# Cluster-routed attention and a long convolution on one core: the output weights' load cut in four, three more idle products, two folded inverses, and a new order

## The chip, the core and the metric

The kernel runs on one core of a Trainium2 chip. Its engines are TensorE (PE, products; PEld are its weight loads), VectorE (DVE), ScalarE (ACT), GpSimd (POOL) and SyncE (SP, which here only issues DMAs). The metric is the device time of one execution in microseconds; lower is better. Every time below is of that kind, and the times inside an execution come from one profiled run.

## What is computed

Four batches, eight heads, 768 positions, 64 columns a head. Every query and key is assigned to one of 16 clusters of its head; a query attends only to keys of its own cluster. The attention's output, 512 columns a position, goes through a gated convolution over all positions:

```python
q_assign = argmax(einsum('bhsd,hcd->bhsc', q_n, c_n))     # q_n, c_n: normalised
k_assign = argmax(einsum('bhsd,hcd->bhsc', k_n, c_n))
mask = q_assign[:, :, :, None] == k_assign[:, :, None, :]
scores = where(mask, q @ k.T / 8, -1e9)
attn = softmax(scores) @ v                                # x[b, s, h*64+d]
x1, x2, x3 = split(x @ w_proj, 3)                         # 512 x 1536
x2_conv = irfft(rfft(x2, axis=1) * rfft(filter_fft, axis=0), axis=1)
y = x1 * x2_conv * x3
out = y @ w_out                                           # 512 x 512, float32
```

## The kernel before

**A planned order.** The kernel is not written in the order in which it runs. Every operation is recorded with `Plan.op` (L94): the engines that may do it with an estimated duration for each, a due time, the keys that it reads and writes, the PSUM bank that it takes or frees. `place` (L123) then puts the operations one by one on the engines: of those that are ready, by due time and estimated start. The table `NUDGE` (L43) holds a shift of the due time for each operation, by its number in the order of recording, and `ONLY` pins some operations to one engine. So these two tables, together with the estimates, set the order of every engine's instructions and of the DMA queues. `COLD` is a constant of the planner's estimates alone: it tells until when TensorE is reckoned to run slow.

**Groups and stages.** The work comes in eight head groups n, two a batch, four heads each. For each group:
- the loads of q and k (L323) and v (L328), by half groups (pair pr of two heads);
- `routing(n)` (L574): transposes of q and k on TensorE (L594, L605), similarities with the centroids (sim, L625) and their transpose (L638), the one-hot of the best cluster (L646 to L663), a DMA transpose of the one-hots (ohT, L668), and eight small DMAs that copy them as mask rows into the score operands (aug<-ohT, L497). The mask is thus part of the score product: a large constant times the one-hots is added in the contraction;
- `attention(n, pr)` (L677): for each of six key tiles three score products of 512 columns (L699, through `product`, L82 for whole 128-column products and L84 for two halves of 64), their exponentials on ACT (L708, L711), and the product with the values (L722). VectorE and POOL sum the exponentials over key tiles: first tiles two at a time (L739, 512 columns, on either engine), then whole tiles (L743, VectorE). The denominators are either a product with ones (L756), or a DMA that folds the sums (acc<-acc, L776, issued by POOL) and two small ones (dd, L780; dp, L782) ahead of a reciprocal and its spread over partitions (rb, L793). The result is scaled into x transposed (xT, L822).

After an odd group its batch is complete, and `hyena(b)` (L830) is recorded; its products fill TensorE between the scores of the next groups: the projection x2 (L856), sums of positions with their mirror (L870, L875), the spectra by products with DFT tables (L475, L84), the product with the filter's spectrum (L886, L890), and then for each of four column tiles dt the projections x3 and x1 (L919 to L930), the inverse transform (L939 to L952), the product y2 of the three (L968), and at last the product with the output weights (L994 to L1012) and the output DMAs (L988, L1007, L1011). The last batch's `hyena` has nothing behind it that could hide it: it is the tail.

**Two forms of the inverse.** A whole inverse takes 16 calls of `product`; its two halves of frequencies (even, odd) are combined inside PSUM, with a negated table `neg` (L894), and VectorE then makes two sums (yy, L965). A folded one takes 8; VectorE makes two sums more (sd, L955) before the two of L965. The copy od (L953) is there in both. `whole = last and dt >= WHOLE` (L898) decides; with `WHOLE = 0` all four of the last batch are whole, and the other batches' are folded.

**The head.** `warm` (L1089) fills a part of the tile wpj with ones and issues `WARM` idle products of 128x128 by 512 columns (L1096), which read nothing else and whose result nobody reads, before the first transposes (L605). `constants` (L1016) loads the DFT tables; the filter's spectrum hm is made on the way (L455 and around).

**The weights.** `weights` (L1078) records four loads of the projection (L1082) and one of the output weights (L1085), all issued by POOL. The tile wout is at first the third DFT table of the filter's spectrum, so its load waits for the last reader of `("fw", 2, ...)`.

**DMAs.** A queue issues in order; an issue whose data or buffer isn't ready holds up what stands behind it. SyncE's queue carries q, k, v, the one-hot transposes, the masks, dd, rb and the outputs; POOL's carries the weights and the folds acc<-acc.

Of the kernel before, what the change touches and what calls it, by code (L numbers as in the profile page):

```python
# [26 lines left out]
ND = DM // 128  # L27
# [10 lines left out]
WHOLE = 0  # L38
# [6 lines left out]
HOLD = {"score": "score", "o": "o"}  # L45
AFTER = {"PE": .16}
TABLE = 1.283
WARM = 7
SOON = 0
RATE = 215e3  # L50
LOAD = 300e3

COLD, SLOW = 6.5, .95
OVERLAP = {"ACT": .09, "DVE": .08}
MODES = {"pv": 64, "bc": 64, "half": 64, "sim": 32, "den": 32, "score": 0, "proj": 0, "inv": 0}


def array(o, last):

# [205 lines left out]
def build(T):  # L265

    P = Plan()
    op = P.op
# [406 lines left out]
    first, prev = [None], []  # L675

    def attention(n, pr, sins):  # L677
# [120 lines left out]
        else:  # L798
# [10 lines left out]
            for ch in range(2):  # L809
# [6 lines left out]
                op(("PE", .95), bc, te + 3, r=["dn"], w=[rk[ch]], alloc=rk[ch], kind="bc")  # L816
        osv = lambda: T.osb[o3][:, :, :384]
        eps = lambda: T.osb[o3][:, 1, 384:385]
        xs = b % 2
        xv = lambda: T.xT[xs][:, kt].rearrange("p (a b) -> p a b", a=2)  # L820
        for a_ in [slice(0, 2)] if not last else [slice(0, 1), slice(1, 2)]:
            op(("DVE", .6 if last else 1.01), lambda e, a_=a_: T.nc.vector.scalar_tensor_tensor(  # L822
                xv()[:, a_], osv()[:, a_], eps(), ap(rk[a_.start])[:, :384].unsqueeze(1) if last else rbv(), op0=Alu.add,
                op1=Alu.mult), te + (4 if last else 12), r=[("osb", o3)] + (rk[a_] if last else rk), w=[("xT", xs, kt)],
               free=rk[a_] if last else [], lock=True)


    INV = [("inv", m) for m in range(2)]

    def hyena(b):  # L830
        xs = b % 2
        last = b == B - 1
        w0 = A(24 * (b + 1)) + 11.84958
        w1 = A(24 * (b + 2)) + 50.56423 if b < B - 2 else A(96) + 35.31752
        if last:
            w0 = A(96) - 4.47412
            w1 = w0 + 10
        acc = [0.0]

        def step(d):  # L840
# [130 lines left out]
        for tt in range(3):  # L971
            ob, obk = (T_("tm", 0), [("tm", 0, 0), ("tm", 0, 1), ("tm", 0)]) if last and tt == 2 else (
                T_("ob", tt % 2), [("ob", tt % 2, 0), ("ob", tt % 2, 1), ("ob", tt % 2)])
            for e_ in range(2):
                due = step(.87)
                if last and tt == 2 and e_:
                    for x in range(2):
                        h, cols = Bank(), ts(x, DM // 2)

                        def half(e, kts, cols=cols, h=h):  # L980
                            for kt in kts:
                                columns(ap(h)[:, :DM // 2], T.y2[:, kt, ts(NT - 1, 128)], T.wout[:, kt, cols], kt == 0, kt == ND - 1)
                        op(("PE", .36), lambda e, half=half: half(e, range(3)), due, r=[("y2", dt) for dt in range(3)] + ["wout"],
                           w=[h], alloc=h, kind="proj")
                        op(("PE", .12), lambda e, half=half: half(e, range(3, 4)), due, r=[("y2", 3), h], w=[h], kind="proj")
                        op({"ACT": .37, "DVE": .42}, lambda e, cols=cols, ob=ob, h=h: copy(e, ob()[:, 1, cols], ap(h)[:, :DM // 2]), due + 1,
                           r=[h], w=[("end", x)], free=[h])
                        op({"ACT": .4, "SP": .4}, lambda e, cols=cols, ob=ob: dma(e)(  # L988
                            T.out[b].rearrange("(p t) m -> p t m", t=NT)[:, NT - 1, cols], ob()[:, 1, cols]), due + 2,
                           r=[("end", x)], byts=78e3)  # L990
                    break
                h = Bank()

                def W(e, kts=range(ND), tt=tt, e_=e_, h=h):  # L994
                    for kt in kts:
                        columns(ap(h), T.y2[:, kt, ts(2 * tt + e_, 128)], T.wout[:, kt], kt == 0, kt == ND - 1)
                if last:
                    op(("PE", .647), lambda e, W=W: W(e, range(3)), due, r=[("y2", dt) for dt in range(3)] + ["wout"],
                       w=[h], alloc=h, kind="proj")
                    op(("PE", .217), lambda e, W=W: W(e, range(3, 4)), due, r=[("y2", 3), h], w=[h], kind="proj")  # L1000
                else:
                    op(("PE", .862), W, due, r=[("y2", dt) for dt in range(ND)] + ["wout"], w=[h], alloc=h,
                       kind="proj")
# [74 lines left out]
    def weights():  # L1078
        op(("POOL", .1), lambda e: T.nc.gpsimd.tensor_copy(T.wpj[0:1, :, 0:1], T.f[1][0:1, 0, 0:4].unsqueeze(2)), 29,
           r=[("f", a, b) for a in range(2) for b in range(2)], w=[("wpj", i) for i in range(ND)])  # L1080
        for i in range(ND):
            op(("POOL", .8), lambda e, i=i: T.nc.gpsimd.dma_start(  # L1082
                T.wpj[:, i], T.w_proj.rearrange("(t p) m -> p t m", p=128)[:, i]), 44 + 13 * i, w=[("wpj", i)], byts=786e3,
               after=[first[0]], kind="load")
        op(("POOL", .8), lambda e: T.nc.gpsimd.dma_start(T.wout, T.w_out.rearrange("(t p) m -> p t m", p=128)), 115,  # L1085
           w=["wout", ("fw", 2, 0), ("fw", 2, 1)], byts=1048e3, after=[first[0]], kind="load")
# [188 lines left out]
```

## Time and profile before

| what | value |
|---|---|
| median of 3 runs | 380.7 us (376.28 to 382.66) |
| profiled execution, its own time | 378.68 us |
| its span in the trace | 376.9 us |
| granted TensorE clock, mean | 0.999 |
| busy: TensorE, VectorE | 363.4 us, 339.2 us |
| busy: ScalarE, GpSimd | 262.7 us, 108.5 us |
| last product ends, output DMAs end | 372.6 us, 376.9 us |
| first group of instructions on TensorE | the seven idle products, 1.45 to 4.62 us |

The span runs from the first to the last record of the trace; the execution's own time is 1.8 us longer. The costliest groups of instructions are the products with the values (L722, 143.1 us in 768 products), the halved products of L84 (69.4 us for the scores alone) on TensorE; the exponentials on ACT (L711 and L708, 109.1 and 57.5 us); and the sums L743 on VectorE (112.3 us in 64). In the lines of the trace an instruction is shown with its start, its duration, engine, line, operation, the tiles that it writes and reads, their shapes and a count, and in brackets the idle time ahead of it and what ended it. A matmul's end is modelled, so a stretch of idle time is read better from start to start.

### The profile page before, as it was taken

The page shows a single profiled execution, that of the slowest core. Times are in us where ns is not written, and L with a number is a line of the kernel's source. Part 1 is how long each engine was busy: PE and PEld are TensorE (multiplying, and loading weights), DVE is VectorE, ACT ScalarE, POOL GpSimd, SP SyncE. Part 2 cuts the span into 40 slices and gives each one's busy share as a digit, 9 for nine tenths or more (in the row PEclk, how much of TensorE's full clock was granted, in tenths as well). Part 3 has the DMA queues.
Part 4 walks back from the last instruction along what each step waited for, and adds up shares of the span by engine and source line. Part 5 has one row for each costly group of instructions (what it writes and reads, how often), then busy time and mean ns, then how long its engine had stood idle before and what let it go on. Part 6 is the DMA issues. An engine that isn't in the chain of part 4 may idle for free.

```text
span 376.9 us, 8462 instructions
## 1 busy us (share of the span) xinstructions
PE 363.4 (96%) x3240; PEld 207.4 (55%) x3242; DVE 339.2 (90%) x507; ACT 262.7 (70%) x490; POOL 108.5 (29%) x153
## 2 busy tenths in 40 slices
PE   7999999999999699999999999999999999999995
PEld 4554445454555355566555556667555565565682
DVE  7889996868899859999998988999899999999992
ACT  7996969786985567769669637889855876433332
POOL 8511102321221642331331144311330252022600
PEclk9999999999999999999999999999999999999999
DMA  8869756682587777869785796748355941120214
GB/s 171 186 122 209 129 129 165 120 193 50 115 178 106 176 147 133 130 127 181 157 114 136 129 208 137 142 98 128 63 77 101 210 85 13 45 101 2 113 57 167
DMA packets 95668, 47.56 MB, mean 126 GB/s; under 512 B 83768, under 2 KB 89612, under 8 KB 95628
## 3 DMA queue, kind: packets, MB, share of 16 engines
q1 hardware_dynamic: 91836, 37.69, 44.4%
q0 software_dynamic: 2704, 8.98, 17.0%
q8 instruction: 25, 0.41, 0.5%
q10 hardware_dynamic: 1088, 0.36, 0.4%
q14 instruction: 15, 0.12, 0.1%
HBM read 31.59 MB, written 7.40 MB: 103 GB/s over the span
## 4 chain that ended last, share of the span: by engine, by line
PE 75%; DVE 11%; DMA 6%; issue 3%; ACT 3%; SPq 2%; DVEq 0%; ACTq 0%
PE pair L722 27%; PE bank L84 27%; PE bank L82 5%; PE bank L856 4%; DVE acc L743 4%; PE bank L594 3%; PE bank L625 2%; DMA vraw<-in_v_dram 2%; PE bank L638 1%; PE bank L605 1%; DMA qkraw<-in_k_dram 1%; DMA rb<-dr 1%; PE bank L756 1%; DMA dd<-acc 1%; DVE hm L455 1%
## 5 line engine op out<-in xcount | busy, mean ns | idle before, releaser
L722 PE MATMUL pair<-p,vraw 128*64 128x385 f32 x768 | 143.1, 490 | 2.6 <-DMA vraw<-in_v_dram 2.5
L711 ACT ACTIVATE p<-bank 128x512 f32<-128x512 f32 x192 | 109.1, 606 | 29.7 <-PE bank L84 24.6
L743 DVE TENSOR_TENSOR acc<-p,acc 128x1536 f32<-128x1536 f32 x64 | 112.3, 1754 | 3.5 <-POOL acc L739 0.8
L722 PEld LDWEIGHTS pair<-p,vraw 128*64 128x64 f32 x768 | 54.8, 136 | 51.9 <-issue 41.7
L84 PE MATMUL bank<-aug,aug 80*64 80x256 bf16 (+3 forms) x626 | 69.4, 326 | 1.0 <-DMA aug<-ohT 0.5
L708 ACT ACTIVATE p<-bank 128x512 f32<-128x512 f32 x96 | 57.5, 606 | 7.7 <-PE bank L84 4.8
L84 PEld LDWEIGHTS <-aug 80*64 80x64 bf16 (+1 forms) x626 | 38.7, 109 | 33.5 <-issue 21.5
L776 POOL DMA_DIRECT2D acc<-acc x30 | 23.8, 792 | 95.3 <-DMA acc<-acc 53.9
L284 POOL CAST aug<-qkP 64x768 bf16<-64x768 f32 x28 | 23.2, 833 | 67.2 <-DVE acc L743 33.6
L84 PE MATMUL bank<-xT,wpj 128*64 128x384 bf16 x392 | 36.2, 326 | 0.0
L282 ACT COPY qkP<-bank 128x512 f32<-128x512 f32 (+1 forms) x46 | 23.6, 550 | 12.7 <-PE bank L594 6.5
L84 PEld LDWEIGHTS <-y 128*64 128x64 bf16 x504 | 24.8, 110 | 13.8 <-issue 5.5
L886 DVE TENSOR_TENSOR tm<-bank,hm 128x512 f32<-128x512 f32 x44 | 27.8, 682 | 4.7 <-PE bank L475 3.2
L890 POOL TENSOR_TENSOR y<-tm 128x512 bf16<-128x512 f32 x19 | 23.9, 1274 | 17.3 <-DVE tm L886 12.9
L84 PEld LDWEIGHTS <-wpj 128*64 128x64 bf16 x392 | 23.1, 110 | 10.4 <-issue 2.6
L739 DVE TENSOR_TENSOR acc<-p,p 128x512 f32<-128x512 f32 x38 | 24.9, 683 | 4.1 <-ACT p L708 2.7
L739 POOL TENSOR_TENSOR acc<-p,p 128x512 f32<-128x512 f32 x10 | 13.4, 1347 | 39.5 <-ACT p L711 25.5
L84 PE MATMUL bank<-wout,y 128*64 128x512 bf16 (+1 forms) x200 | 22.8, 370 | 0.0
L856 PE MATMUL bank<-wpj,xT 128*64 128x512 bf16 x192 | 22.1, 379 | 0.0
L282 ACT CAST aug<-qkP 64x768 bf16<-64x768 f32 x24 | 19.8, 830 | 2.3 <-PE bank L84 1.5
L282 ACT COPY ob<-bank 128x512 f32<-128x512 f32 x19 | 10.8, 591 | 13.2 <-PE bank L84 12.9
L746 ACT COPY osb<-pair 128x770 f32<-128x770 f32 x16 | 12.8, 802 | 9.5 <-PE pair L722 9.4
(171 smaller groups left out, 465.3 us busy)
## 6 DMA issues: line engine op xcount, KB each, us to landing
vraw<-in_v_dram SPq DMA_DIRECT2D x16, 384.0 KB, 4.2
qkraw<-in_k_dram SPq DMA_DIRECT2D x30, 192.0 KB, 4.0
qkraw<-in_q_dram SPq DMA_DIRECT2D x30, 192.0 KB, 4.5
rb<-dr SPq DMA_DIRECT2D x30, 192.0 KB, 3.6
out_dram<-ob SPq DMA_DIRECT2D x11, 512.0 KB, 3.0
acc<-acc POOLq DMA_DIRECT2D x10, 384.0 KB, 5.1
acc<-acc POOLq DMA_DIRECT2D x10, 192.0 KB, 4.2
y<-in_moe_filter_fft_dram SPq DMA_DIRECT2D x4, 384.0 KB, 6.6
```

Of the source, the lines that this page charges most:

```text
L84: T.nc.tensor.matmul(out[64 * i:64 * i + 64], lhsT[:, 64 * i:64 * i + 64], rhs, start=start, stop=stop)
L282: T.nc.scalar.copy(out, in_)
L284: (T.nc.vector if e == "DVE" else T.nc.gpsimd).tensor_copy(out, in_)
L708: T.nc.scalar.activation(o, ap(h).rearrange("p (a b) -> p a b", a=2), Act.Exp, scale=0.125)
L711: T.nc.scalar.activation(flat(s)[:, lo:lo + 512], ap(h), Act.Exp, scale=0.125)
L722: T.nc.tensor.matmul(o[64 * hp:64 * hp + 64, ch, :385], T.vraw[vs][:, hp, sk * D:(sk + 1) * D], T.p[slots[sk]][:, hp, 384 * ch:384 * ch + ...
L739: alu(e).tensor_tensor(o, x, y, op=Alu.add)
L743: T.nc.vector.tensor_tensor(T.acc[os], T.p[slots[sk]][:, :, :S], T.acc[os], op=Alu.add)
L776: op(("POOL", .8), lambda e, rows=rows: T.nc.gpsimd.dma_start(flat_()[:rows], flat_()[rows:2 * rows], accum_op=Alu.add), te, r=[], w=AK, b ...
L856: T.nc.tensor.matmul(ap(h)[64 * i:64 * i + 64], T.xT[xs][:, kt, c:c + 64], T.wpj[:, kt, DM:2 * DM], start=kt == 0, stop=kt == ND - 1)
L886: op(("DVE", .68), lambda e, i=i, cs=cs, r=r, h=h: T.nc.vector.tensor_tensor(T.tm[r][:, cs], ap(h), hmrow(i, (0, 2, 2, 3)[2 * r + cs]), op ...
L890: op({"POOL": 1.5, "DVE": .68}, lambda e, i=i, r=r: alu(e).tensor_tensor(T.y[:, i, r], T.tm[r][:, 0], T.tm[r][:, 1], op=Alu.add if r else ...
```

## The change

- The load of the output weights, one operation, becomes four of a quarter each (128 rows), with due times 118, 125, 132 and 139 in place of 115. Only the first takes over the third DFT table's keys. The products that read the weights now name four keys.
- `WARM` goes from 7 to 10.
- `WHOLE` goes from 0 to 2: the inverses dt = 0 and 1 of the last batch are folded, 2 and 3 stay whole.
- `COLD`, the planner's constant, goes from 6.5 to 7.2.
- `NUDGE` and `ONLY` are new throughout: other shifts for all operations, and other pinned ones. In the first hundred operations, for instance, `ONLY` before pins 10, 11, 13, 15 to POOL, 14 to ACT and 27 to 30 and 32 to 37 to SP; after, 10 and 12 to 15 to POOL, 26, 27, 30 and 34 to SP and 32, 38 and 41 to ACT.

```diff
-WHOLE = 0
+WHOLE = 2
...
-NUDGE = {0:-687.781,1:-3670.067,2:5.217,3:4.307,4:36.296, ...
-ONLY = {10:"POOL",11:"POOL",13:"POOL",14:"ACT",15:"POOL", ...
+NUDGE = {0:-457.288,1:-646.784,2:-12.57,3:-12.571,4:-1.604, ...
+ONLY = {10:"POOL",12:"POOL",13:"POOL",14:"POOL",15:"POOL", ...
...
-WARM = 7
+WARM = 10
...
-COLD, SLOW = 6.5, .95
+COLD, SLOW = 7.2, .95
...
+    WOUT = [("wout", i) for i in range(ND)]
...
-                        op(("PE", .36), ..., r=[("y2", dt) for dt in range(3)] + ["wout"],
+                        op(("PE", .36), ..., r=[("y2", dt) for dt in range(3)] + WOUT,
...
-        op(("POOL", .8), lambda e: T.nc.gpsimd.dma_start(T.wout, T.w_out.rearrange("(t p) m -> p t m", p=128)), 115,
-           w=["wout", ("fw", 2, 0), ("fw", 2, 1)], byts=1048e3, after=[first[0]], kind="load")
+        for i in range(ND):
+            op(("POOL", .8), lambda e, i=i: T.nc.gpsimd.dma_start(
+                T.wout[:, i], T.w_out.rearrange("(t p) m -> p t m", p=128)[:, i]), 118 + 7 * i,
+                w=[("wout", i)] + [("fw", 2, 0), ("fw", 2, 1)] * (i == 0), byts=262e3, after=[first[0]], kind="load")
```

(The same replacement of `["wout"]` by `WOUT` stands in the two other operations with the output weights.) The diff alone does not tell where an instruction comes to stand; that follows from the listed order of each engine's instructions in the two kernels.

More of the change, by code (lines that the diff above doesn't have):

```diff
@@ L43 @@
-ONLY = {10:"POOL",11:"POOL",13:"POOL",14:"ACT",15:"POOL",27:"SP",28:"SP",29:"SP",30:"SP",32:"SP",33:"SP",34:"SP",35:"SP",36:"SP",37:"SP",44:"ACT",62:"ACT",63:"DVE",64:"POOL",66:"DVE",69:"POOL",91:"POOL",96:"ACT",98:"DVE",152:"ACT",223:"POOL",224:"POOL",229:"DVE",236:"POOL",241:"POOL",352:"POOL",354:"POOL",403:"DVE",404:"POOL",405:"POOL",407:"DVE",408:"DVE",409:"DVE",410:"POOL",412:"DVE",457:"POOL",458:"POOL",494:"ACT",544:"DVE",559:"DVE",560:"DVE",573:"POOL",585:"ACT",588:"DVE",590:"POOL",596:"DVE",614:"ACT",635:"POOL",684:"DVE",685:"ACT",686:"ACT",687:"POOL",689:"ACT",692:"DVE",693:"DVE",694:"DVE",695:"DVE",696:"POOL",698:"POOL",701:"DVE",804:"POOL",856:"POOL",859:"POOL",864:"POOL",867:"POOL",984:"POOL",1007:"ACT",1014:"POOL",1015:"POOL",1016:"DVE",1065:"DVE",1070:"ACT",1140:"DVE",1144:"POOL",1145:"POOL",1149:"DVE",1152:"ACT",1153:"POOL",1154:"DVE",1312:"POOL",1313:"POOL",1323:"DVE",1367:"DVE",1369:"DVE",1416:"ACT",1472:"DVE",1493:"DVE",1497:"ACT",1501:"DVE",1504:"ACT",1516:"POOL",1526:"ACT",1529:"ACT",1531:"DVE",1599:"ACT",1602:"ACT",1607:"POOL",1608:"POOL",1610:"POOL",1612:"DVE",1613:"ACT",1647:"POOL",1648:"DVE",1767:"POOL",1868:"DVE",1899:"ACT",1907:"ACT",1920:"ACT",1927:"DVE",1935:"DVE"}
@@ new lines @@
+ONLY = {10:"POOL",12:"POOL",13:"POOL",14:"POOL",15:"POOL",26:"SP",27:"SP",30:"SP",32:"ACT",34:"SP",38:"ACT",41:"ACT",50:"DVE",62:"ACT",64:"POOL",69:"POOL",90:"DVE",91:"POOL",94:"DVE",97:"DVE",98:"POOL",173:"POOL",174:"DVE",175:"DVE",223:"DVE",224:"DVE",229:"DVE",230:"POOL",235:"DVE",241:"ACT",242:"POOL",245:"ACT",323:"DVE",355:"POOL",357:"POOL",392:"ACT",405:"POOL",406:"DVE",408:"POOL",410:"DVE",411:"DVE",412:"DVE",414:"DVE",415:"POOL",419:"ACT",460:"POOL",462:"POOL",497:"DVE",512:"DVE",539:"DVE",547:"DVE",550:"DVE",563:"DVE",573:"ACT",580:"ACT",588:"ACT",595:"ACT",599:"DVE",607:"POOL",617:"ACT",687:"ACT",688:"ACT",689:"ACT",690:"DVE",692:"POOL",693:"DVE",695:"ACT",696:"DVE",697:"ACT",698:"POOL",699:"POOL",700:"ACT",701:"POOL",703:"DVE",704:"DVE",807:"POOL",808:"DVE",860:"ACT",861:"ACT",870:"ACT",915:"DVE",916:"DVE",988:"POOL",1010:"ACT",1048:"DVE",1051:"ACT",1066:"DVE",1068:"ACT",1095:"POOL",1146:"POOL",1147:"POOL",1152:"DVE",1154:"POOL",1155:"ACT",1156:"DVE",1312:"ACT",1313:"DVE",1314:"DVE",1315:"POOL",1317:"ACT",1372:"DVE",1419:"DVE",1424:"ACT",1452:"POOL",1492:"ACT",1500:"ACT",1505:"POOL",1519:"DVE",1603:"ACT",1604:"ACT",1605:"ACT",1610:"POOL",1611:"POOL",1612:"POOL",1770:"POOL",1772:"DVE",1882:"DVE",1889:"DVE",1934:"DVE",1939:"ACT",1942:"ACT"}
@@ L982, in half @@
                                 columns(ap(h)[:, :DM // 2], T.y2[:, kt, ts(NT - 1, 128)], T.wout[:, kt, cols], kt == 0, kt == ND - 1)
-                        op(("PE", .36), lambda e, half=half: half(e, range(3)), due, r=[("y2", dt) for dt in range(3)] + ["wout"],
+                        op(("PE", .36), lambda e, half=half: half(e, range(3)), due, r=[("y2", dt) for dt in range(3)] + WOUT,
                            w=[h], alloc=h, kind="proj")
@@ L997, in hyena @@
                 if last:
-                    op(("PE", .647), lambda e, W=W: W(e, range(3)), due, r=[("y2", dt) for dt in range(3)] + ["wout"],
+                    op(("PE", .647), lambda e, W=W: W(e, range(3)), due, r=[("y2", dt) for dt in range(3)] + WOUT,
                        w=[h], alloc=h, kind="proj")
@@ L1001, in hyena @@
                 else:
-                    op(("PE", .862), W, due, r=[("y2", dt) for dt in range(ND)] + ["wout"], w=[h], alloc=h,
+                    op(("PE", .862), W, due, r=[("y2", dt) for dt in range(ND)] + WOUT, w=[h], alloc=h,
                        kind="proj")
```

2 lines of the change are left out of this document (1 added, 1 removed).

## The prediction, made before the changed kernel had run

> **What bounds the kernel now.** I read the page's first two parts, then the span cut into stages, then TensorE's waits, and then the queues around the one stage in which TensorE is slack.
>
> ```profile
> span 376.9 us, 8462 instructions
> PE 363.4 (96%) x3240; PEld 207.4 (55%) x3242; DVE 339.2 (90%) x507; ACT 262.7 (70%) x490; POOL 108.5 (29%) x153
> PE   7999999999999699999999999999999999999995
> ```
>
> TensorE is busy for 96% of the span, and the row of 40 slices (9.4 us each) has three low digits: the first, the one at 122 to 132 us, and the last. VectorE, at 90%, is second by little.
>
> ```profile
> core 0: us, PE busy (x) PEld busy (x) DVE busy (x) ACT busy (x) POOL busy (x), PEclk, DMA share, GB/s
> 0.00:20.00 20.00, 16.56 (x105) 9.77 (x106) 16.86 (x44) 17.21 (x32) 12.71 (x54) 1.00 0.95 173
> 120.00:132.00 12.00, 8.97 (x78) 4.68 (x76) 10.54 (x16) 7.86 (x14) 6.14 (x7) 1.00 0.74 155
> 132.00:340.00 208.00, 207.37 (x1870) 121.44 (x1869) 193.85 (x287) 145.40 (x272) 59.72 (x62) 1.00 0.63 120
> 340.00:372.60 32.60, 32.53 (x420) 21.47 (x416) 29.33 (x50) 11.90 (x23) 9.15 (x7) 1.00 0.17 68
> 372.60:376.90 4.30, 0.00 (x0) 0.00 (x0) 0.00 (x0) 0.40 (x2) 0.00 (x0) 0.90 0.61 231
> ```
>
> From 132 to 372.6 us TensorE lacks 0.7 us in all, so nothing is won there unless its work shrinks. The idle time lies in the head (3.4 us), at 120 to 132 (3.0 us), and behind the last product (4.3 us: output DMAs). From 20 to 120 us it is busy for 98.0 of 100. TensorE's waits by what ended them (us in total, times, longest):
>
> ```profile
> PE pair L722 <- DMA vraw<-in_v_dram: 2.5, 1, 2.5
> ...
> PE bank L605 <- DMA qkraw<-in_k_dram: 1.2, 1, 1.2
> PE bank L756 <- DVE hm L455: 0.7, 1, 0.7
> PE bank L84 <- DMA aug<-ohT: 0.5, 1, 0.5
> ```
>
> The largest wait is one load of values, and the mask wait (aug<-ohT) stands in the same stage. SyncE's queue tells why:
>
> ```profile
> 110.25 1.28 SPq L668 DMA_TRANSPOSE ohT<-oh  x1
> 118.02 5.30 SPq L497 DMA_DIRECT2D aug<-ohT  x8
> ...
> 124.78 0.63 SPq L328 DMA_DIRECT2D vraw<-in_v_dram  x1
> ```
>
> The one-hot transpose of group 3, issued at 110.25, takes 7.7 us to land (median of the seven such rows 4.4). Two us before it, POOL had issued the 512 KB output weights:
>
> ```profile
> 108.26 0.86 POOL L1085 DMA_DIRECT2D wout<-in_moe_w_out_dram  x1
> ```
>
> That load takes 8.6 us to land, over the whole of the transpose. The eight mask copies wait for the transpose and hold SyncE's queue until 123.3; the values of group 3 stand behind them. TensorE then runs dry twice:
>
> ```profile
> 124.02 0.84 PE L84 MATMUL bank<-aug,aug 80*64 80x512 bf16 x8 [0.53 <-DMA aug<-ohT]
> 131.53 1.52 PE L722 MATMUL pair<-p,vraw 128*64 128x385 f32 x8 [2.50 <-DMA vraw<-in_v_dram]
> ```
>
> Counted by starts (start of a product to start of the next, less the usual pitch of its shape), the two cost 0.8 and 2.8 us. That is more than the bracketed idle, since modelled ends run on.
>
> **The change, part by part.**
>
> *Weights in quarters.* One issue on POOL becomes four of 128 KB, +3 issues by 0.86 = 2.6 us of POOL, which is busy for 29%. The due values are later, but in the listed order of the new kernel the issues stand earlier: two behind the aug cast that follows the fourth wpj load (its neighbours run at 86 to 87 us before), two behind the L739 sum at 94, all ahead of the first fold acc<-acc (L776, at 107.41 before, just ahead of the old load). So the weights should be in the chip by about 100. The third DFT table shares their tile; its last reader is long past in both orders. Group 3's transpose then meets no such load: 7.7 falls to 4.4 (−3.3), and its one-hot ends after 17 instead of 20 L743 sums (1.754 us each on VectorE), thus earlier. On SyncE's queue the values of group 3 are moved ahead of transpose and masks, straight behind group 2's masks; they wait there only for the buffer that the products of group 1's second pair free, before 100 us. What can be late next is the mask: by its distance from the last sim products it has 19.1 us of TensorE work against 16.7 before, so I take no new wait. Gain between 0 (another transfer takes the place) and 3.6; I take 3.4, as both causes move in the same direction and the sum of the stalls is known.
>
> *Fifties.* At 53.8 TensorE waits for the L455 filter rows ahead of the first denominators; by starts 2.6 us are lost between 50 and 60. In the new order these denominators stand behind the scores and one product with values, and one L743 (1.75) stands behind the L455 rows which free the banks. The banks come 1.75 sooner, but scores need them sooner too. Between +1 and −2.6; I take −0.6, near the end that keeps the wait, for the rows still stand there.
>
> *Head.* The seven idle products start 0.427 apart (from 1.45); three more end at about 1.45 + 10 × 0.427 = 5.7. The first transposes, now at 4.62, wait anyway from 5.49 to 6.71 for a load of k (1.22 us). So +1.28 of TensorE's work is covered by that wait if the loads land as they do now. If the covering wait went, it would cost up to 1.28. The loads themselves are reordered between ACT and SyncE, and the first sim copies go about 0.6 later on ACT (a sine and a cast stand before). I take +0.1; bounds −1.5 and +1.3. The lower bound is the pace: transposes of 128x128 start 0.24 apart until about 10.4 and 0.147 apart at 12.2, so some 15 of them at 0.1 each are to be had if the full pace came earlier. In the new order TensorE is not idle between 1.45 and the first transposes, a stretch that is broken at 5.49 now.
> [...]
>
> *Two folded inverses.* In the last batch two of the four inverses go from 16 to 8 pairs of half products each. The eight banks of the present ones take 5.28 us (356.69 to 361.97), 0.081 a pair of half products (64 pairs in all). So 16 pairs fewer are −1.3 us of TensorE at the very end, where it has no slack. VectorE gains 4 sums sd L955 (547 ns, 24 in the trace) = +2.19.
>
> *Tail.* VectorE has no idle time in it from 338 on:
>
> ```profile
> 366.12 0.94 DVE L968 TENSOR_TENSOR y<-yy,qkP 128x768 bf16<-128x768 f32 x1
> 366.98 1.02 DVE L928 TENSOR_TENSOR qkP<-bank,qkP 128x384 f32<-128x384 f32 x2
> 368.04 0.96 DVE L968 TENSOR_TENSOR y<-sim,qkP 128x768 bf16<-128x768 f32 x1
> 369.61 0.69 DVE L284 COPY tm<-bank 128x512 f32<-128x512 f32 x1 [0.61 <-PE bank L84]
> ```
>
> The last L968 ends at 369.0, and the products that need it start at about 369.25: 0.25 of slack. Behind the last xT (L822) the new order gives VectorE +2.2 (L955), +0.5 (L965), +1.0 (L822), +0.5 (L928) and −0.6 (a copy), together +3.6, less 0.3 for overlap between successive rows: +3.3. TensorE has 32.8 us of work there ahead of those products, 31.9 before, and 2.28 behind them, 3.25 before. Thus TensorE waits 3.3 − 0.9 − 0.25 = 2.1, of which about 0.4 is given back where POOL takes one L965 (the order has it there): 1.7. With the fold's −1.3 the tail is +0.4. Bounds: −1.3 (the wait hidden, if VectorE reaches the last L822 earlier) and +2.6.
>
> *New order elsewhere.* Totals by listed counts and mean durations: VectorE 0, ACT +2.3, POOL +5.8, TensorE 0 (1.28 − 1.29). At 0.7 us of slack in 208 I take 0; bounds −1 and +4.
>
> Sum: 376.9 − 3.4 − 0.6 + 0.1 + 0.4 = 373.4 of span, and 1.8 us lie around the span in the profiled execution (378.68 − 376.9): **375.2**. The profiled execution is 2.0 below the median of the runs shown (380.7; 376.28 to 382.66), so on the median's footing this reads 377.
>
> **Rivals.**
>
> A, the sum, 375.2; its bounds on the single steps give 372 to 378.5.
>
> [...]
>
> C, the stall keeps its size in another place: the quarters, issued at 86 to 97, meet group 2's loads or its transpose (4.4 becomes 7.7 there), and masks or values of that group are 3.4 late: 375.2 + 3.4 = 378.6, no change. For it: the DMA share is 0.67 from 20 to 120 already. Against it: four parts of a quarter's size leave gaps, and the wpj loads, 384 KB each, ran in that stretch without a stall.
>
> D, slower: VectorE becomes the bound. From 140 to 370 it is idle for about 11 us, of which POOL's longer list can eat up some: an L739 on POOL takes 1347 ns against 683, four more of them stand there, and each L743 behind one waits; 4 × 1.35 = 5.4, plus 3.3 in the tail, against TensorE's 0.25 of slack: 375.2 + 5.4 + 3.3 = 384 (379 to 391). It decides as soon as VectorE reaches the last L822 later than now by more than 0.25 against TensorE. For it: the busy share of 93% from 132 to 340. Against it: the L739 wait row is 0.8 us in the whole trace.
>
> **How the numbers follow.** A 0.42, B 0.25, C 0.15, D 0.18. A change of 2% (7.6 us) is about what a measurement of this kernel can tell from none, its runs lying 1.7% apart. Faster by that means below 373.1: most of B (0.21) and a quarter of A (0.10): 0.31. Slower means above 388.3: half of D, 0.09. Else 0.60. The range of 368 to 386 leaves out B's lowest tenth part, half of D and little else, less than 0.2; A's own is 372 to 378.5.
>
> **What would show it.** The profile after should have no wait of L722 for vraw at 120 to 132 and a full digit there; ohT of group 3 landing in about 4.4; four wout issues by 100 us. The idle products should end at 5.7 with little wait behind them; the denominators in the fifties should stand behind scores. In the tail, eight pairs fewer in each folded inverse and a wait of 1 to 2 us ahead of the last L84 bank<-wout,y products. [...]

## The result, and the profile after

| | before | changed |
|---|---|---|
| median of 20 runs each, us | 376.25 (374.31 to 384.48) | 377.60 (376.29 to 379.95) |
| ratio | 1 | 1.0043, 95% interval 1.0025 to 1.0061 |
| profiled execution, own time / span | 378.68 / 376.9 | 378.54 / 376.8 |

The change makes the kernel 0.4% slower: no change by the 2% bound, but clear of the noise, and the other way than the forecast of 375.2. Runs of disturbed executions are left out of the ratio.

The two profiled executions are equal to 0.1 us. They aren't two usual ones, though: that of before lies 2.4 us above its kernel's median, that of the changed kernel 0.9. Set beside the three runs that the prediction had (median 380.7), the first one had looked a little short.

The profile of the changed kernel, the lines that answer to those shown of before; first the page:

```profile
span 376.8 us, 8529 instructions
PE 363.2 (96%) x3253; PEld 209.1 (55%) x3257; DVE 341.1 (91%) x509; ACT 263.9 (70%) x492; POOL 113.7 (30%) x156
PE   6899998999999999999999999999999999999994
PEclk9899999999999999999999999999999999999999
```

The low digit at 122 to 132 us is gone. The stages:

```profile
core 0: us, PE busy (x) PEld busy (x) DVE busy (x) ACT busy (x) POOL busy (x), PEclk, DMA share, GB/s
0.00:20.00 20.00, 15.79 (x101) 8.25 (x102) 15.52 (x41) 16.25 (x29) 13.29 (x55) 0.91 0.96 173
120.00:132.00 12.00, 12.00 (x103) 7.28 (x99) 11.41 (x17) 9.40 (x16) 5.32 (x6) 1.00 0.74 146
132.00:340.00 208.00, 206.40 (x1902) 123.48 (x1901) 196.78 (x289) 147.58 (x277) 62.12 (x62) 1.00 0.60 116
340.00:372.60 32.60, 31.40 (x384) 19.75 (x380) 29.50 (x51) 12.41 (x25) 10.43 (x9) 1.00 0.17 66
372.60:376.90 4.30, 0.00 (x0) 0.00 (x0) 0.00 (x0) 0.00 (x0) 0.00 (x0) 0.94 0.62 239
```

TensorE is busy for all of 120 to 132 (8.97 of 12 before): the stall that the prediction wanted gone is gone. But the last row but one lacks 1.2 us where it lacked 0.1, and in the head the granted clock is 0.91. Its waits:

```profile
PE bank L594 <- DVE hm L455: 0.9, 1, 0.9
PE bank L462 <- DVE qkP L284: 0.9, 1, 0.9
PE bank L353 <- DVE sd L350: 0.7, 1, 0.7
PE bank L605 <- DMA qkraw<-in_q_dram: 0.7, 1, 0.7
PE bank L82 <- DVE hm L455: 0.7, 2, 0.4
...
PE bank L84 <- DVE sd L956: 0.5, 2, 0.3
```

No wait for values is left. In its place stand small ones: for hm in the fifties (0.9 and 0.7; 0.7 before), for VectorE in the head, for sd (the folded inverse's sum) in the tail. From 132 to 340 TensorE lacks 1.6 us, where it lacked 0.6.

**Where the time went, stage by stage.** For each execution I took what TensorE loses in a stage: from start to start of its products, less their usual pitch by shape, as in the prediction. Before: the mean over four further profiles of the unchanged kernel (own times 376.40 to 376.96; experiments 1, 9, 15, 16). After: the mean over four executions that share the changed kernel's order there (the profile above, experiments 5, 8 and 12; experiment 12, which writes less, is left out of the last row but one). What counts as the usual pitch is a choice; with another one single rows move by up to 0.3 us, and none above 0.3 changes its sign.

| stage, us | first profile of before | before, usual | changed | difference |
|---|---|---|---|---|
| 0 to 20, with the idle products | 12.73 | 13.09 | 13.18 | +0.1 |
| 20 to 50 | 2.21 | 2.41 | 2.39 | 0.0 |
| 50 to 60 | 2.34 | 2.34 | 2.75 | +0.4 |
| 60 to 120 | 2.94 | 3.26 | 2.71 | -0.55 |
| 120 to 140 | **3.52** | **1.21** | 1.08 | -0.1 |
| 140 to 340 | 7.48 | 6.93 (6.63 to 7.54) | 7.72 (6.99 to 8.25) | +0.8 |
| 340 to the last product | 0.21 | 0.21 | 1.10 | +0.9 |
| products saved by two folded inverses | | 0 | -1.32 | -1.3 |
| start of the last product to the end | 4.63 | 4.62 | 5.31 | +0.7 |
| sum | | | | +0.9 |

The sum is +0.9 of the 1.35 measured between the medians; the row 140 to 340 scatters by more than the rest. Two places carry the answer: the stage of the stall lost 3.5 us in the one profile that the prediction read and 1.2 on the mean of the others, and the tail gives back what the fold saves.

### The profile page after: what moved, and what is told of

It reads as the page before. It is cut to its first block, busy times and chain, and to the rows that moved or that the text cites. A ratio compares the mean times of both kernels' runs of the same rounds, so it can differ in the third digit from the quotient of the medians.

```text
span 376.8 us, 8529 instructions
## 1 busy us (share of the span) xinstructions
PE 363.2 (96%) x3253; PEld 209.1 (55%) x3257; DVE 341.1 (91%) x509; ACT 263.9 (70%) x492; POOL 113.7 (30%) x156
## 4 chain that ended last, share of the span: by engine, by line
PE 69%; DVE 13%; ACT 7%; DMA 4%; issue 3%; SPq 2%; POOL 1%; DVEq 0%; POOLq 0%; ACTq 0%
PE pair L722 28%; PE bank L84 24%; PE bank L594 5%; PE bank L82 3%; PE bank L625 2%; PE bank L857 2%; DMA dn<-dd 2%; PE bank L638 2%; DVE tm L887 1%; DVE tm L871 1%; ACT aug L282 1%; SPq L497 1%; DMA aug<-ohT 1%; ACT p L711 1%; DMA dd<-acc 1%
## 5 line engine op out<-in xcount | busy, mean ns | idle before, releaser
L743 DVE TENSOR_TENSOR acc<-p,acc 128x1536 f32<-128x1536 f32 x64 | 113.5, 1774 | 10.9 <-POOL acc L739 5.8
L84 PE MATMUL bank<-aug,aug 128*64 128x512 bf16 (+3 forms) x650 | 70.7, 325 | 1.4 <-DMA aug<-ohT 0.5
L84 PEld LDWEIGHTS <-aug 128*64 128x64 bf16 (+1 forms) x650 | 39.6, 109 | 35.2 <-issue 24.8
L84 PE MATMUL bank<-xT,wpj 128*64 128x384 bf16 x456 | 43.3, 326 | 0.0
L84 PEld LDWEIGHTS <-wpj 128*64 128x64 bf16 x456 | 27.7, 110 | 13.7 <-issue 5.2
L284 POOL CAST aug<-qkP 64x768 bf16<-64x768 f32 x23 | 19.3, 842 | 52.3 <-DVE acc L743 21.0
L739 POOL TENSOR_TENSOR acc<-p,p 128x512 f32<-128x512 f32 x14 | 18.1, 1297 | 48.5 <-DVE acc L739 26.0
L891 POOL TENSOR_TENSOR y<-tm 128x512 bf16<-128x512 f32 x17 | 21.5, 1277 | 20.2 <-DVE tm L887 12.3
L282 ACT CAST aug<-qkP 64x768 bf16<-64x768 f32 x28 | 23.1, 830 | 1.4 <-PE bank L84 0.6
L746 ACT COPY osb<-pair 128x770 f32<-128x770 f32 x16 | 12.9, 804 | 14.6 <-PE pair L722 14.4
L739 DVE TENSOR_TENSOR acc<-p,p 128x512 f32<-128x512 f32 x34 | 22.6, 693 | 0.3 <-ACT p L711 0.3
```

What stands on the lines that cost most here:

```text
L84: T.nc.tensor.matmul(out[64 * i:64 * i + 64], lhsT[:, 64 * i:64 * i + 64], rhs, start=start, stop=stop)
L282: T.nc.scalar.copy(out, in_)
L284: (T.nc.vector if e == "DVE" else T.nc.gpsimd).tensor_copy(out, in_)
L739: alu(e).tensor_tensor(o, x, y, op=Alu.add)
L743: T.nc.vector.tensor_tensor(T.acc[os], T.p[slots[sk]][:, :, :S], T.acc[os], op=Alu.add)
L891: op({"POOL": 1.5, "DVE": .68}, lambda e, i=i, r=r: alu(e).tensor_tensor(T.y[:, i, r], T.tm[r][:, 0], T.tm[r][:, 1], op=Alu.add if r else ...
```

## Experiments

In all of them only the named instructions differ; the order of every other instruction is kept as planned. Ratios are to the kernel before, run on the same chip; intervals 95%.

**1, 9, 15, 16: the kernel before, unchanged, profiled again.** No edit.

> The kernel before, unchanged, profiled once more. Its 20 runs have a median of 376.25 us, 2.4 below the profiled execution of the prediction (378.68). Theory 1 (the stall at 120 to 132 us belonged to that one execution): no wait of L722 for vraw above 0.5 us there, the transpose of group 3 lands in about 4.4 instead of 7.7 us, and the own time is about 376. Theory 2 (the stall is in every execution, and the changed kernel loses what it wins elsewhere): the same wait of about 2.5 us and about 3.4 us lost from 120 to 132.

> The kernel before, unchanged, a third profile. If the wait for the values at 120 to 132 us is not in its usual execution: about 0.3 us lost between 120 and 140 (3.5 in the first profile), no such wait, own time within 1 us of 376.3. If it comes in every second execution: the wait again, and about 378.5.

> The kernel before, unchanged, a fourth profile, to see how the loss between 120 and 140 us goes with the execution's own time. If the stall makes the long executions: its loss there is below 2 us where the own time is below 377.5, and above 3 us where it is above 378.5. If long executions have other causes: no such relation.

> The kernel before, unchanged, a fifth profile, with the same two expectations as the fourth.

Own times 376.55, 376.82, 376.40 and 376.96. Lost from 120 to 140 in experiments 1, 9, 15 and 16: 0.32, 1.87, 1.97 and 0.69, against 3.52 in the first profile (378.68). The wait for the values is absent in three of the four and 0.9 in experiment 15. So not all of that loss is the stall; most of the 1.87 of experiment 9 is another chain, a score behind an exponential, behind a sum on POOL, behind the small DMA dd<-acc, which still reads what the sum writes:

```profile
134.56 1.78 POOL L739 TENSOR_TENSOR acc<-p,p 128x512 f32<-128x512 f32 x1 [2.01 <-DMA dd<-acc]
136.38 2.07 ACT L711 ACTIVATE p<-bank 128x512 f32<-128x512 f32 x4 [2.34 <-POOL acc L739]
137.02 0.41 PE L84 MATMUL bank<-aug,aug 128*64 128x512 bf16 x2 [1.07 <-ACT p L711]
```

In experiment 1, TensorE around the place of the old stall:

```profile
128.44 0.87 PE L84 MATMUL bank<-aug,aug 80*64 80x512 bf16 x8
129.12 1.49 PE L722 MATMUL pair<-p,vraw 128*64 128x385 f32 x8
130.41 1.06 PE L84 MATMUL bank<-aug,aug 80*64 80x512 bf16 x10
```

and SyncE's queue in the same execution:

```profile
111.22 1.28 SPq L668 DMA_TRANSPOSE ohT<-oh  x1
117.92 5.21 SPq L497 DMA_DIRECT2D aug<-ohT  x8
...
124.59 0.63 SPq L328 DMA_DIRECT2D vraw<-in_v_dram  x1
```

Masks and values are issued at the same times as in the first profile to 0.2 us (values at 124.59, there 124.78). The transpose was issued 1.0 later and took 6.7 instead of 7.7, the weights 8.0 instead of 8.6. And yet the product with the values starts at 129.12 with no wait; in the first profile it starts at 131.53. The values had landed by 129.1 here, that is 4.5 us after the issue, and at 131.5 there, 6.7 after.

Experiments 10, 11 and 13 below change only the tail, so their profiles are three more executions of this stage. All eight, by how long the transpose of group 3 took to land, with TensorE's bracketed waits:

| execution | own time | transpose, us | wait for masks | wait for values |
|---|---|---|---|---|
| 11 | 376.31 | 6.5 | 0 | 0 |
| 16 | 376.96 | 6.6 | 0 | 0 |
| 1 | 376.55 | 6.7 | 0 | 0 |
| 9 | 376.82 | 6.9 | 0 | 0 |
| 13 | 377.26 | 7.0 | 0.11 | 1.09 |
| 15 | 376.40 | 7.5 | 0.15 | 0.86 |
| first profile | 378.68 | 7.7 | 0.53 | 2.50 |
| 10 | 382.77 | 9.7 | 2.23 | 2.45 |

The two waits of experiment 10 in its list of TensorE's waits:

```profile
PE pair L722 <- DMA vraw<-in_v_dram: 2.4, 1, 2.4
PE bank L84 <- DMA aug<-ohT: 2.2, 1, 2.2
```

The weights' load lies over the transpose each time (7.9 to 8.7 us to land), but TensorE waits only where the transpose took 7.0 us or more, and most where it took longest. Why it takes longer in one execution than in another isn't shown. Theory 1 holds for the usual time, not in its wording: the transpose takes 6.6 to 7.5 us in these four, not 4.4, and one wait is 0.9. The expectation of experiments 15 and 16 that the stall makes the long executions isn't contradicted: below 377.5 no execution loses more than 2.0 us in the stage, and the two above 378.5 wait 3.0 and 4.7 us there. Two long ones are few, and below 377.5 the loss and the time don't go together.

**2: before, its one load of the weights earlier.**

```diff
-order:  ... wpj 3, aug, acc<-acc, wout, acc<-acc ...
+order:  ... wpj 3, wout, aug, acc<-acc, acc<-acc ...
```

> The kernel before with its one load of the output weights moved on POOL's queue straight behind the fourth load of the projection (some 10 us earlier), every other instruction of every engine in the same order. Theory 1 (stall of one execution): within 0.3 us of before, since there is nothing to win in most runs. Theory 2 (real stall, made by the load over the one-hot transpose): 2.4 to 3.4 us faster, ratio 0.991 to 0.994, with the wait of L722 for vraw gone. A third outcome, the load in that place costs something of its own (the fold DMAs or POOL's sums behind it): up to 1 us slower.

376.53 us, ratio 1.0003 (0.9985 to 1.0022): nothing, as theory 1 said. In its profile the transpose of group 3 lands in 2.8 us and there is no wait at the old place; but 2.2 us are lost at 100 to 120 (0.3 in the others), 1.2 of them a wait for an earlier load of values. That profiled execution (378.55) is the longest of its twelve runs, so it doesn't tell whether the usual one has merely moved the collision.

**3: changed kernel, the four quarters later.**

```diff
-order:  ... wout 0, wout 1, acc<-p4,p0, wout 2, wout 3, acc<-acc ...
+order:  ... acc<-p4,p0, acc<-acc, wout 0, wout 1, wout 2, wout 3 ...
```

> The changed kernel with its four quarter loads moved back behind the first fold acc<-acc, where the load stood before; every other instruction in the same order. If the earlier place of the weights removed the stall: 2 to 3.4 us slower than the changed kernel (ratio to before about 1.010 to 1.013), with a wait for masks or values at 120 to 132. If the new order of SyncE's queue (values ahead of the transpose, the one-hot earlier) removed it, or the stall was of one execution: ratio to before the changed kernel's 1.004, no such wait.

379.63 us, ratio 1.0093 (1.0060 to 1.0126): 0.5% above the changed kernel's own 1.0043 (1.0025 to 1.0061), with intervals that just touch. In its profile, the fastest of its runs, 2.3 us are lost at 120 to 140 (1.1 in the changed kernel), with a wait of 1.2 for a qkraw load; masks and values aren't waited for, so neither expectation names what happened. In this profile the new order alone keeps the old stall away, since the transpose (issued at 102.59) is ahead of the weights (108.67); the late weights then meet other loads. By the ratios the early place is worth about 1.9 us in the new order, and nothing in the old (experiment 2).

**4: changed kernel with seven idle products.**

```diff
-            for _ in range(WARM):
+            for _ in range(7):
```

> The changed kernel with seven idle products instead of ten, every other instruction in the same order. If the three more idle products are hidden behind the waits of the first transposes: ratio to before unchanged at 1.004, first scores at the same time. [...] If they bring the pace earlier and lose it again in the half clock seen from 11.6 to 14.3 us of the changed kernel's profile: 0 to 0.7 us faster, ratio 1.002 to 1.004, with no half clock in the head.

378.14 us, ratio 1.0053 (1.0032 to 1.0073), not told apart from 1.0043. Idle products and losses up to 20 us come to 2.99 + 10.08 = 13.07 us, against 4.27 + 8.82 = 13.09 in experiment 5: the three more are hidden. The full pace of TensorE begins at 10.9 us in it and at 7.0 in experiment 5, so an earlier full pace is worth nothing here.

**5: changed kernel, profiled again.** No edit.

> The changed kernel, unchanged, profiled once more, to tell what belongs to its usual execution. Theory (the small losses are in every execution): about 2.9 us lost from 50 to 60 us, about 1 us from 340 to 370, about 1 us from 120 to 140; a half clock in the head perhaps, perhaps not. Rival (they belong to the profiled execution, as the old stall did): two of the three gone, time about 376.5.

376.51 us. 2.7 lost from 50 to 60, 1.1 from 120 to 140 and 1.1 from 340 on, as in the first profile (2.9, 1.1, 1.1): the small losses belong to the order, not to the execution. The half clock in the head (last section) is not there this time.

**6: changed kernel, all four inverses whole.**

```diff
-            def I(...): if whole:
+            def I(...): if last:
-                sd = bank0 + od, bank0 - od; yy from sd
+                yy from bank0 and od, at the place of the sd sums
```

> The changed kernel with all four inverses of the last batch whole again; the two sums of VectorE that follow each stand where the sd sums stood, the four others fall away; the order is else the same. If the fold saves 1.3 us of TensorE and gives back 0.9 us in waits for VectorE at the end: 0.4 us slower than the changed kernel, ratio to before 1.005. If the added sums on VectorE cost more than the products saved: 0.5 to 1 us faster, ratio 1.002. If the waits in the tail come from elsewhere and stay: 1.3 us slower, ratio 1.008.

377.98 us, ratio 1.0047 (1.0023 to 1.0070), against an expected 1.005; from the end of the last xT to the end of the kernel 39.61 us, against 38.92. So the fold pays about 0.7 of the 1.3 us that it takes off TensorE; the ratio alone would not show it.

**7: changed kernel, one sum behind the filter rows.**

```diff
-VectorE: ... L455 h, L743 acc<-p0, L455 hm x2, L453, L455 hm x2, L284 qkP x3 ...
+VectorE: ... L455 h, L455 hm x2, L453, L455 hm x2, L743 acc<-p0, L284 qkP x3 ...
```

> The changed kernel with one L743 sum (1.75 us, at 52.84 in its profile) moved on VectorE's queue behind the last L455 row; nothing else. If the loss from 50 to 60 is made by the banks that the L455 rows free late: 0.9 to 1.7 us faster than the changed kernel (ratio to before 0.9995 to 1.002), waits for hm gone. If the exponentials or the scores are next to wait (their buffers are freed by that sum): within 0.3 us, with the wait named otherwise.

380.42 us, ratio 1.0107 (1.0070 to 1.0144): slower by 0.6%, and neither expectation named the way. VectorE and TensorE in it:

```profile
53.86 1.41 DVE L455 SCALAR_TENSOR_TENSOR hm<-bank,hw,tm 128x512 bf16<-128x512 f32 x2 [1.25 <-ACT tm L451]
```

```profile
59.77 0.38 PE L82 MATMUL bank<-aug,aug 80*128 80x512 bf16 x1 [0.83 <-DVE qkP L284]
60.96 0.81 PE L82 MATMUL bank<-aug,aug 80*128 80x256 bf16 x4 [0.82 <-DVE qkP L284]
```

The rows wait 1.25 us for a scaled copy that ACT makes, so that only 0.3 of the 1.75 us is won (against the reciprocal ahead of them); then the moved sum stands ahead of the copies of q and k out of PSUM, the scores wait for those banks, and 5.3 instead of 2.6 us are lost from 60 to 100. Not all of that is waiting. Behind these waits the granted clock (third figure from the end) falls:

```profile
62.00:64.00 2.00, 2.00 (x12) 0.44 (x12) 1.18 (x2) 1.94 (x4) 0.74 (x1) 0.57 1.13 214
64.00:66.00 2.00, 2.00 (x18) 0.62 (x18) 0.47 (x1) 0.03 (x1) 1.98 (x3) 0.58 0.54 66
```

From 62.3 to 65.7 TensorE runs at half clock, two products with the values start 0.64 apart (62.52 and 63.16) instead of 0.32, and some 1.6 of the 2.7 us more are lost there. Experiment 5 has no such fall. So the stage has three limits close together. Whether the other five runs had the half clock too isn't known, and that the waits brought it on isn't shown.

**8: changed kernel, one of the last two output DMAs from SyncE.**

```diff
-ACT: copy tm, out tm 0, out tm 1
+ACT: copy tm, out tm 1          SyncE: out tm 0
```

> The changed kernel with one of the last two output DMAs issued by SyncE instead of ACT, which issues both in a row (372.38, 1.13 us for the two); nothing else. If that second issue ends the kernel: 0.4 to 0.6 us faster, ratio to before 1.003. If the copies on ACT or the transfer itself end it: no difference, 1.004.

377.37 us, ratio 1.0028 (1.0004 to 1.0052), which takes in both expectations; in the trace the end lies 7.55 us behind the last y2 (7.56 to 7.58 without the edit). By the trace, the last issue does not set the end.

**12: changed kernel, 512 KB of the last output not written.**

```diff
-                op(("SP", .4), lambda e, tt=tt, ob=ob: T.nc.sync.dma_start(
+                op(("SP", .4), lambda e, tt=tt, ob=ob, last=last: last and tt == 1 or T.nc.sync.dma_start(
```

> The changed kernel without one of the last batch's three output transfers (512 KB of 1.57 MB are not written); everything else as it is. If the outputs' transfer fills the end (1.57 MB at about 400 GB/s from 0.8 us behind its first issue): about 1.2 us faster than the changed kernel, ratio to before 1.001, and the end 6.3 instead of 7.56 us behind the last y2. If the last issue and its landing set the end: no difference, 1.004.

376.74 us, ratio 1.0010 (0.9980 to 1.0040), 1.001 expected; in the trace the end comes 6.59 us behind the last y2 instead of 7.56. At some 400 GB/s these 512 KB are 1.3 us, and 0.97 came off: the transfer sets most of the end. The windows of the last microseconds, experiment 1 (before) and experiment 5 (changed):

```profile
369.00:370.00 1.00, 1.00 (x14) 0.66 (x12) 0.22 (x1) 0.59 (x2) 0.00 (x0) 1.00 1.00 389
370.00:371.00 1.00, 0.39 (x8) 0.12 (x4) 0.20 (x1) 0.86 (x2) 0.00 (x0) 1.00 0.99 397
371.00:372.00 1.00, 0.00 (x0) 0.00 (x0) 0.00 (x0) 0.00 (x0) 0.00 (x0) 1.00 0.84 311
```

```profile
369.00:370.00 1.00, 0.68 (x12) 0.33 (x6) 0.28 (x1) 1.00 (x3) 0.00 (x0) 1.00 0.82 311
370.00:371.00 1.00, 0.00 (x0) 0.00 (x0) 0.14 (x1) 0.31 (x2) 0.00 (x0) 1.00 1.01 406
371.00:372.00 1.00, 0.00 (x0) 0.00 (x0) 0.00 (x0) 0.00 (x0) 0.00 (x0) 1.00 1.04 418
```

The last two columns are the DMA engines' busy share and GB/s. In the changed kernel TensorE ends 0.7 us sooner, but the DMA engines are full (share about 1, some 400 GB/s) either way, and both spans end at 374.7. The last batch's 1.57 MB all wait for the last y2, since every output product needs it. Behind the last y2, TensorE's last product starts 1.0 us sooner in the changed kernel (2.2 against 3.2 us behind it), and only 0.3 of that comes off the end (7.56 against 7.88).

**10, 11, 13, 14: the tail taken apart.** The time from the end of the last xT (L822) to the end of the last y2 (L968) is VectorE's chain: in it VectorE is busy for all but 0.8 us, before and after.

> The kernel before with the inverses dt = 0 and 1 of the last batch folded (its four sd sums stand on VectorE's queue right ahead of the two that follow); everything else in its order. If the last y2 of VectorE ends the tail (it has no idle time from the last xT on): about 1.9 us slower, ratio 1.005, the last y2 about 31.6 us behind the last xT instead of 29.7. If TensorE ends it: 1.3 us faster, ratio 0.9965.

> The kernel before with 2.2 us taken off VectorE in the tail (two copies out of PSUM go to ACT, the product y2 of dt = 0 to POOL) and with one inverse folded (TensorE -0.66, VectorE +1.1); else its order. If VectorE's last y2 ends the tail: 0.6 to 1 us faster than before, ratio 0.9975, the last y2 about 28.8 us behind the last xT. If the outputs' transfer or TensorE ends it: within 0.3 us, 1.000.

> As the earlier run with relief in the tail (two copies to ACT, y2 of dt = 0 to POOL, one inverse folded, the order of before), but the product on POOL reads a tile of its own, so that VectorE's next sums don't wait for it (they waited 1.99 us). If VectorE's chain to the last y2 sets the end: the last y2 about 28.6 us behind the last xT (29.7 before, 30.55 in the earlier run), 0.7 to 1.1 us faster than before, ratio 0.997 to 0.998. If not: within 0.3 us of before.

> The changed kernel with y2 of dt = 0 moved from VectorE (0.96 us) to POOL, with a tile of its own; everything else in its order. If VectorE's chain sets the end: the last y2 30.4 to 30.7 us behind the last xT (31.36), 0.6 to 0.9 us faster than the changed kernel, ratio to before about 1.002. If TensorE sets it by now: within 0.3 us, 1.004.

```diff
 experiment 10, before:          emit the inverses dt = 0, 1 folded
 experiment 11, before:          emit dt = 0 folded; od and one ob copy: DVE -> ACT; y2 of dt = 0: DVE -> POOL
 experiment 13:                  as 11, and the folded sums of dt = 0 in a tile of their own (T.p[0])
 experiment 14, changed kernel:  y2 of dt = 0: DVE -> POOL, with a tile of its own
```

| | last xT to last y2 | last xT to the end | ratio |
|---|---|---|---|
| before (6 executions) | 29.57 to 29.69 | 37.45 to 37.56 | 1 |
| 10: before, two folded | 32.10 | 39.93 | 1.0053 (1.0026 to 1.0079) |
| 11: before, relief | 30.55 | 38.38 | 1.0035 (1.0005 to 1.0066) |
| 13: before, relief, own tile | 29.03 | 36.90 | 0.9981 (0.9947 to 1.0014) |
| changed (3 executions) | 31.36 to 31.37 | 38.92 to 38.95 | 1.0043 |
| 14: changed, y2 on POOL | 30.66 | 38.31 | 1.0021 (0.9979 to 1.0062) |

In experiment 10 one of the two last sums of dt = 1 stands ahead of the sd sums that it should read, so that it reads what stood there before; the instructions are as many. Its profiled execution is the long one of the table above; what it lost there lies ahead of the last xT, outside the stretch measured here. Over all six rows the end follows the last y2 by 7.55 to 7.88 us. Folding in the old order costs 0.5%, though it takes 1.3 us off TensorE. Experiment 11 missed its expectation, and shows why:

```profile
358.92 1.02 DVE L969 TENSOR_TENSOR yy<-bank,od 128x384 f32<-128x384 f32 x2 [1.99 <-POOL y L972]
```

The slower POOL (1.81 us for this product, VectorE 0.96) still read the tile that VectorE's next sums write. With a tile of its own (experiment 13) the chain is some 0.6 shorter than before and the end 0.6 sooner, a little under the expected 0.7 to 1.1. Its ratio, 0.9981, is the lowest here (376.03 us, against 377.57 of before on the same chip), but the interval takes in 1, so it is shown to be faster in the tail only. Experiment 14 likewise takes 0.7 us off the changed kernel's chain and 0.6 off its end, as expected for VectorE's chain; its interval is too wide for more.

## Why the prediction was wrong, point by point

**Weights in quarters, -3.4: the step that failed.** Its reading of the queues was right (the quarters issued at 88.28 and 97.31; values ahead of the masks; no wait), and the stage's loss did go to 1.1. Its mechanism stands too: the longer the transpose under the weights' load, the longer the waits for masks and values in the old order (no wait at 6.5 to 6.9 us, 4.7 us of waits at 9.7); in the nine profiles with the new order there is none at that place. What failed is the amount. The stall was read from one execution, and "the sum of the stalls is known" was true of that execution only: the two waits came to 3.0 us in it, to 0, 0, 0 and 1.0 in experiments 1, 9, 16 and 15. In these four the stage loses 0.3 to 2.0 us, so the change wins about 0.1 there on their mean. It should win more in executions as long as the first, which a median hardly sees; no run here measures that. A remainder of 1.1 in the new order (about 0.5 of it one score that waits for an exponential, at 131 to 133) had not been seen. The prediction saw the gap between this execution and the median, but the median of three pointed the wrong way: the kernel's median of twenty runs is 2.4 below the profiled execution, not 2.0 above. That its "377 on the median's footing" lies near the measured 377.6 is luck, since that footing was over 4 us too high.

**Fifties, -0.6: wrong sign.** +0.4. The denominators went behind the scores as listed, but the banks' rows were no earlier for the next reader; experiment 7 shows the limits behind (ACT's scaled copy, then the copies of q and k). The bound of +1 held it.

**Head, +0.1: right.** +0.1, the idle products hidden, experiment 4. Its pace of the transposes was misread, 0.24 and then 0.147 apart for 0.21 (until 9.9) and 0.11 (from 12.35), with the same difference of 0.1. A full pace that comes sooner is there as well: in the changed kernel transposes start 0.11 apart from 5.65 on in the first profile and from 6.97 in experiment 5; in the first profile of before they are 0.21 apart until 9.9. It pays nothing, since TensorE then waits for the loads and VectorE (from start to start about 1.0 and 1.1 us in a row in the first profile, 1.2 and 1.1 in experiment 5); the first profile:

```profile
5.51 0.84 PE L605 MATMUL bank<-ident,qkraw 128*128 128x128 f32 x6 [0.31 <-DMA qkraw<-in_k_dram]
7.06 0.97 PE L605 MATMUL bank<-ident,qkraw 128*128 128x128 f32 x6 [0.71 <-DMA qkraw<-in_q_dram]
8.77 0.30 PE L353 MATMUL bank<-ident,sd 128*64 128x128 f32 x1 [0.74 <-DVE sd L350]
8.91 0.82 PE L605 MATMUL bank<-ident,qkraw 128*128 128x128 f32 x6
10.58 0.32 PE L462 MATMUL bank<-fw,identr 64*64 64x384 bf16 x1 [0.85 <-DVE qkP L284]
```

**Fold and tail, +0.4: the size right by luck, its parts not.** Measured +0.9 in waits, -1.3 in products, +0.7 behind the last product: +0.3. VectorE's instructions behind the last xT grew by 2.1 us, not 3.6 (52 there, 48 before), or by 1.6, not 3.3, with their overlap taken off, and TensorE's wait is 0.9, not 1.7. The time behind the last product is no term of the sum, so it was taken to stay; it grew by 0.7, for the end is bound by the last y2 and the transfer (experiment 12), so that products saved behind that y2 are hardly paid. The term to carry into the sum was the chain's: +1.68 to the last y2.

**New order elsewhere, 0.** -0.55 from 60 to 120, and about +0.8 from 140 to 340, which scatters by 1.3. Part of the second has an address: in all four executions of the changed kernel two scores wait behind VectorE's sd sums of an earlier batch (L956, near 254 and 268, about 0.4 each by starts) and one for masks near 293 (0.3 to 0.8), where before has one wait for an exponential (near 254, 0.5). The rest stays open.

**Rivals.** C (the gain is eaten elsewhere, no change) comes nearest by its time, not by its mechanism: no other transfer was 3.4 late. D was right that VectorE binds in the tail; its L739 sums cost VectorE waits of 1.4 us behind 140, not 5.4, and no wait of TensorE names them. B, at 0.25, counted on a gain from a sooner full pace, and no run shows that gain: in experiment 4 the full pace begins at 10.9 us instead of 7.0, and idle products and losses up to 20 us come to as much (13.07 us against 13.09). The 377.6 lies in the stated range of 368 to 386 and in A's 372 to 378.5 by their width alone, since the time moved the other way.

## What to carry to other kernels

A wait in one profile is a sample: before a gain is booked for its removal, look at the same stage in further executions, and set the profiled one against many runs, not three. A wait on a DMA's landing is the first suspect (the one for the values ran from 0 to 2.5 us over eight executions), also where it stands two engines back (experiment 9); the losses behind other engines' instructions in the fifties and the tail (hm, sd) repeat to 0.2 us. At the end of a kernel follow the chain back from the last bytes: here VectorE's last product releases all of the last outputs, so that TensorE's saved work paid about half and a folded inverse in the old order cost time. And when work goes to a slower engine, see who writes the tile that it still reads (1.99 us of waiting in experiment 11).

## What the runs showed of the hardware

The pace of TensorE in the head is not the same from run to run of one kernel, and it can fall again. In the first profile of the changed kernel the granted clock, in windows of 2 us:

```profile
8.00:10.00 2.00, 0.99 (x8) 0.82 (x8) 1.86 (x8) 1.99 (x5) 2.00 (x3) 1.00 1.31 216
10.00:12.00 2.00, 1.42 (x7) 0.47 (x8) 1.96 (x5) 1.98 (x6) 0.26 (x3) 0.79 1.24 211
12.00:14.00 2.00, 2.00 (x10) 0.77 (x5) 0.29 (x1) 1.75 (x4) 0.82 (x1) 0.50 1.26 213
14.00:16.00 2.00, 2.00 (x16) 1.21 (x16) 1.74 (x4) 1.70 (x5) 0.59 (x1) 0.85 0.03 4
```

(The third figure from the end is the clock.) It is at half from about 11.2 to 14.6, after TensorE had been idle for half of 8 to 10; the pairs of half products of L512 start 0.62 apart there, 0.32 in experiment 5, whose clock stays at 1.00 with the same idle stretches. The unchanged kernel has it too (0.50 from 8.6 to 12.0 in experiment 1), and experiment 7 a second time, from 62.3 to 65.7. It lasts 3.4 us each time. In as long a stretch ahead of these falls TensorE isn't idle throughout: it is busy for 1.82 us (changed kernel), 1.37 (experiment 1) and 1.76 (experiment 7, the second); in experiment 5 for 1.78 from 6.97 to 10.38, with no fall. The longest idle stretch ahead of it is about 1 us in the changed kernel and 1.6 in experiment 1. So the idle time ahead does not tell an execution with a fall from one without, and what brings the fall on isn't shown.

The three more idle products do bring the full pace (transposes 0.11 instead of 0.21 apart, idle products 0.216 instead of 0.427) sooner: in the eight profiles with ten of them it begins at 4.3 to 7.0 us, in the ten with seven at 5.0 to 5.8 four times and at 10.1 to 12.9 six times. The column of the clock doesn't show that: it reads 1.00 from the start in the first profile of before, whose transposes run at half pace until 9.9.
